# Small contexts of two batches at once, in attention over pooled keys followed by a mixture of experts

## The chip, the cores and the metric

The kernel runs on one core of one Trainium2 chip. The metric is the time of one execution on the device, in microseconds (us). The core's engines are TensorE (PE; its weight loads are shown as PEld), VectorE (DVE), ScalarE (ACT), GpSimd (POOL) and SyncE (SP). Each works through its own instructions in order, and semaphores tie them together. PE writes to PSUM, which has eight banks; a bank holds 512 float32 columns on each of 128 partitions.

## The reference

Attention over pooled keys and values, then a dense mixture of experts over all tokens.

```python
# attention: batch 8, heads 8, sequence 576, head size 64, pooled by 8 to 72 keys
k_p = k.reshape(B, H, Sp, pool, D).mean(axis=3)
v_p = v.reshape(B, H, Sp, pool, D).mean(axis=3)
scores = scale * np.matmul(q, k_p.transpose(0, 1, 3, 2))
attn = np.exp(scores - np.max(scores, axis=-1, keepdims=True))
attn = attn / (np.sum(attn, axis=-1, keepdims=True) + 1e-09)
attn_out = np.matmul(attn, v_p)
...
# mixture: x is attn_out as 4608 tokens x 512, 4 experts, hidden size 1024
p = domain_probs / (domain_probs.sum(-1, keepdims=True) + 1e-09)
for e in range(E):
    h = np.maximum(x @ w1[e], 0.0)
    out += p[:, e:e + 1] * (h @ w2[e])
```

## The kernel before

**Chunks.** A batch has 576 = 512 + 64 queries. The first 512 of each batch make a chunk of 512 tokens, chunks 0 to 7. The last 64 of all eight batches make a ninth, chunk 8, kept in `x_rem`. Every chunk goes through the four experts. For each pair of chunk and expert the up product (512 x 512 by 512 x 1024, then relu) and the down product (512 x 1024 by 1024 x 512, times a probability, added to `acc`) are each done by seven products of half-size matrices, with sums of quarters formed by VectorE (`hidden_sums`, `x_sums`, `combine` at L246).

**Slots.** From chunk 1 on an order written out by hand runs: a loop over slots g (L1072), seven to a pair of chunk and expert, 28 to a chunk. A slot issues, in this order: hidden sums on VectorE; step g % 7 of the up product of unit 0 and step (g - 1) % 7 of that of unit 1 (eight 256-column matmuls at L695 together); step (g - 1) % 7 of the down product of the pair before (eight 256-column matmuls at L763); then the pieces of attention work planned for that slot. With `manual_schedule` each engine keeps this order.

**Banks.** PSUM holds `att` (two banks, for attention), `units` (two units of two banks, for the up product) and `chains` (two banks named o_ps, for the down product). A unit's step 0 is copied by ScalarE from its bank 0 to its bank 1 (L708). Step 1 grows bank 1 and is read by ScalarE's relu (L712), steps 4 and 6 use bank 1 and are read by VectorE (`relu_sum`, L675), steps 2, 3 and 5 use bank 0 and are read by ScalarE (L710, L716). So a unit's bank 1 is not in use between the relu of step 1 and step 4. In the down product step 0's bank is copied by ScalarE to the other (L771), once the adds of the pair before have left that one, and step 1 grows the copy. Most results are added to `acc` by VectorE, two instructions to a step (`add`, L842).

**Attention work.** `pieces_later` (L966) plans it per batch b, counted from slot 28 x (b - 2): for b = 2 its own numbers, for b = 3 to 7 mostly those of `usual`, for b = 8, where only the small part of batches 6 and 7 is left, a variant. `context` (L460) multiplies the exponentials of 128 queries (72 keys x 128 queries as weights) with a head's pooled values and a column of ones (65 columns), for 8 heads, into `att`. `divide` (L424) takes the reciprocal of the ones' column and multiplies.

**The small part.** At every even b from 2 on, for visit i = b // 2 - 1, the 64 last queries of batches 2i and 2i + 1 are handled together. `rem_queries` transposes them by a transfer. `rem_scores` (L496) makes 16 products of 64 columns into `att`, and ScalarE takes the exponential of all at once into `expTr` (L510), a batch at a time: first the four head pairs of one batch, then those of the other. `rem_context` (L513) makes 16 products at L520, one per head and batch, with 64 columns of weights each: the first batch's results go to partitions 0 to 63 of `att`, the second's to 64 to 127. `divide` follows, and `rem_turn` transposes into `x_rem` by a transfer on SP's queue. `usual` puts these four at slots -3, 17, 24 and 25, b = 2 at 0, 7, 8 and 14, b = 8 at -3, 17, 21 and 22. The pooled values of three batches are kept in three tiles `vps`, batch b in number b % 3, written by `values_folds`.

Of the kernel before, what the change touches and what calls it, by code (L numbers as in the profile page):

```python
# [10 lines left out]
ALU = mybir.AluOpType  # L11
AX = mybir.AxisListType
BF16 = mybir.dt.bfloat16
F32 = mybir.dt.float32
# [3 lines left out]
def kernel(  # L18
# [10 lines left out]
    nc = tc.nc  # L29

    B, H, S, D = q.shape
    E, DM, F = moe_w1.shape
    P = nc.NUM_PARTITIONS
    NPAIR = H // 2
    POOL = 8
    SP = S // POOL
    NT = 512
    NR = NT // P
    REM = S - NT
# [8 lines left out]
    const = ctx.enter_context(tc.tile_pool(name="const", bufs=1))  # L48
# [3 lines left out]
    apool = ctx.enter_context(tc.tile_pool(name="apool", bufs=1))  # L52
    xpool = ctx.enter_context(tc.tile_pool(name="xpool", bufs=2))
    npool = ctx.enter_context(tc.tile_pool(name="npool", bufs=2))
# [10 lines left out]
    att = psum.tile([P, 2, NT], F32, name="att")  # L65
    units = [None, None]
# [27 lines left out]
    SPT = -(-SP // 16) * 16  # L94
    kp_all = const.tile([SPT, H, 2, D], BF16, name="kp")
    kpTs = [const.tile([P, H + 1, SPT], BF16, name=f"kpT{i}") for i in range(3)]
    vps = [const.tile([SP, H, D + 1], BF16, name=f"vp{i}") for i in range(3)]
    raw_k = rawpool.tile([SP, H, 2, D], BF16, name="kraw")
    raw_v = rawpool.tile([SP, H, 2, D], BF16, name="vraw")

# [89 lines left out]
    def load_q_rem(b):  # L190
        if b % 2 == 0:
            q_rems[b // 2] = qpool.tile([P, H, D], BF16, name="q_rem", bufs=2)
        lo = (b % 2) * REM
        nc.gpsimd.dma_start(
            out=q_rems[b // 2][lo:lo + REM],
            in_=q[b, :, NT:S, :].rearrange("h p d -> p h d"),
        )
# [50 lines left out]
    state = {}  # L248
# [22 lines left out]
    def fold_wide(what, part):  # L271
        raw, wide = ((raw_k, wide_k), (raw_v, wide_v))[what]
        a, *others = (wide[:, :, 2 * i:2 * i + 2, :] for i in range(wide.shape[2] // 2))
        if part == 0:
            for other in others:
                nc.vector.tensor_add(out=a, in0=a, in1=other)
        else:
            nc.vector.tensor_add(out=raw[:], in0=raw[:], in1=a)
# [68 lines left out]
    def queries(b):  # L347
        state[("qT", b)] = apool.tile([P, H, 2, P], BF16, name="qT")
        nc.sync.dma_start_transpose(
            out=state[("qT", b)][:].rearrange("p h a t -> p (h a) t"),  # L350
            in_=raws[("q", b)][:].rearrange("p h r d -> p (h r d)"),
        )
# [27 lines left out]
    def key_columns(b, h, lo):  # L380

        h = h if b else h // 2
        return state[("kpT", b)][:].rearrange("p h j -> p (h j)")[lo:lo + D, h * SPT:h * SPT + P]
# [40 lines left out]
    def divide(c_ps, x_tok):  # L424

        n = c_ps.shape[1]
        c = c_ps[:, :, 0:NPAIR * (D + 1)].rearrange("p a (h d) -> p a h d", d=D + 1)
        inv = npool.tile([P, 2, NPAIR], F32, name="inv")[:, 0:n]
        nc.vector.reciprocal(out=inv, in_=c[:, :, :, D])
        nc.vector.tensor_tensor(  # L430
            out=x_tok[:], in0=c[:, :, :, 0:D],
            in1=inv.unsqueeze(3).to_broadcast([P, n, NPAIR, D]), op=ALU.mult,
        )
# [61 lines left out]

    def rem_scores(i):  # L496
        qTr = state.pop(("qTr", i))
        scr_ps = att[:].rearrange("p h (b a t) -> p h b a t", b=2, a=NPAIR)
        for bb in range(2):
            for pair in range(NPAIR):  # L500
                for hh in range(2):
                    lo = hh * D
                    nc.tensor.matmul(
                        scr_ps[:, hh, bb, pair, :],
                        lhsT=key_columns(2 * i + bb, 2 * pair + hh, lo),
                        rhs=qTr[lo:lo + D, pair, bb, :],
                        skip_group_check=True,
                    )
        expTr = apool.tile([SP, 2, 2, NPAIR, REM], BF16, name="expTr")
        nc.scalar.activation(out=expTr[:], in_=scr_ps[0:SP], func=ACT.Exp, scale=EXP_SCALE)  # L510
        state[("expTr", i)] = expTr

    def rem_context(i):  # L513
        expTr = state.pop(("expTr", i))
        x_tok = npool.tile([P, 2, NPAIR, D], BF16, name="x_tok", bufs=4)
        c_ps = att
        for h in range(H):
            at = h % NPAIR * (D + 1)
            for bb in range(2):
                nc.tensor.matmul(  # L520
                    c_ps[bb * REM:(bb + 1) * REM, h // NPAIR, at:at + D + 1],
                    lhsT=expTr[:, h % 2, bb, h // 2, :], rhs=vps[(2 * i + bb) % 3][:, h, :],
                    skip_group_check=True,
                )
        divide(c_ps, x_tok)
        state[("xr", i)] = x_tok

    def rem_turn(i):
# [140 lines left out]
    def x_sum(c, n):  # L669
        if n == 0:  # L670
            state[("x_sums", c)] = x_sums(c)
        state[("x_sums", c)][n]()
# [293 lines left out]
    def pieces_later():  # L966


        at, amid = {0: [lambda: x_sum(1, 3)]}, {}

        def put_amid(slot, piece):
            amid[slot] = piece

        def put(slot, *pieces):
            at.setdefault(slot, []).extend(pieces)

        usual = dict(
            queries=-8, keys=-9, values=-2, scores=((2, 2), (9, 2)), contexts=(11, 14, 18, 21),
            q=1, k=(-2, 0, 5, 9), v=(-2, 0, 5, 9), x=(22, 25, 25, 25), rem=(-3, 17, 24, 25),
        )  # L980
        plans = {b: usual for b in range(BUSY, B + 1)}
        plans[BUSY] = dict(
            queries=0, keys=4, values=12, scores=((9, 2), (12, 1), (15, 1)), contexts=(16, 17, 19, 21),
            q=6, k=(5, 8, 11, 14), v=(13, 16, 19, 26), x=(24, 25, 25, 25), rem=(0, 7, 8, 14),
        )
        plans[B] = dict(usual, x=(24, 24, 25, 25), rem=(-3, 17, 21, 22))
        plans[BUSY + 1] = dict(usual, keys=-8, turned=-6, values=4, v=(5, 8, 12, 16))

        for b, plan in plans.items():
            start = 7 * E * (b - BUSY)  # L990

            def put_each(what, pieces):
                for slot, piece in zip(plan[what], pieces, strict=True):
                    put(start + slot, piece)

            if b == BUSY:
                put(start + 1, lambda: fold_wide(0, 0))
                put(start + 4, lambda: fold_wide(0, 1))
                put(start + 5, lambda: load_q_rem(BUSY))
                put(start + 8, lambda: fold_wide(1, 0))  # L1000
                put(start + 12, lambda: fold_wide(1, 1))
            if b < B:
                put(start + plan["queries"], lambda b=b: queries(b))
                put(start + plan["keys"], lambda b=b: fold_keys(b))
                put(start + plan.get("turned", plan["keys"] + (b > BUSY)), lambda b=b: keys(b, every))
                put(start + plan["values"], *values_folds(b))
                pair = 0
                for slot, n in plan["scores"]:
                    if n == 2:
                        put(start + slot, lambda b=b, pair=pair: scores_of_two(b, pair))  # L1010
                        put_amid(start + slot + 1, lambda b=b, pair=pair: scores(b, pair, 1))
                    else:
                        put(start + slot, lambda b=b, pair=pair: scores(b, pair))
                    pair += n

                for r, slot in zip((2, 3, 0, 1), plan["contexts"]):
                    put(start + slot, lambda b=b, r=r: context(b, r))
                    put(start + slot + 1, lambda b=b, r=r: turn(b, r))
            if b + 1 < B:
                put(start + plan["q"], lambda b=b: load_q(b + 1), lambda b=b: load_q_rem(b + 1))  # L1020
                for what in range(2):
                    put_each("kv"[what], [lambda b=b, what=what, part=part: load_part(b + 1, what, part)
                                          for part in range(NR)])
            if b % 2 == 0:
                i = b // 2 - 1
                put_each("rem", [lambda i=i, do=do: do(i)
                                 for do in (rem_queries, rem_scores, rem_context, rem_turn)])
            put_each("x", [lambda b=b, n=n: x_sum(b, n) for n in range(4)])
        return at, amid

    ENG = mybir.EngineType
    with tc.manual_schedule(
# [30 lines left out]

        N = len(order)
        later, amid = pieces_later()
        below_of = [(0, 3)] + order
        sums = {}
# [4 lines left out]
        for g in range(7 * N + 1):  # L1072
            t, i = divmod(g, 7)
# [53 lines left out]
```

## Time and profile before

| what | us |
|---|---|
| median of 3 runs | 489.60 (489.58 to 489.82) |
| the profiled execution | 489.93 |
| its span, from the first to the last instruction | 488.2 |
| PE busy in the span | 480.5 (98%) |
| PEld, DVE, ACT, POOL busy | 409.4, 376.9, 303.8, 119.4 |
| the four small contexts L520 start at | 82.4, 216.4, 319.8, 415.7 |
| the divisions L430 out of `att`, 33 of them, each | 0.69 |

The granted TensorE clock is 0.999 of the full one. A share of busy time is a mean over the whole execution. In the timelines a row is: start and duration in us, engine, line, operation, the tile written and those read, the shape, the number of instructions merged, and in brackets the idle time in front with what ended it. In the chain of work in order of time a row is start, duration, engine, tile, line and number of instructions; a piece there begins where the one before it ends, so its start lies a little behind that of the timeline. The shape of a matmul is weights, rows x columns, then the moving operand, rows x columns.

### The profile page before, as it was taken

The numbers are of one execution on the slowest core, as the hardware profiler recorded it, in microseconds if no ns is written. First come the engines' busy times: TensorE is split into PE (matmuls) and PEld (weight loads), VectorE is DVE, ScalarE is ACT, GpSimd is POOL, SyncE is SP. The second block draws the span as 40 slices with busy tenths as digits, with TensorE's granted clock in tenths as the row PEclk, the third lists the DMA queues.
The fourth block names the chain that finished last, engine by engine and source line by source line (L and its number), as shares of the span: only waits on it lengthen the run. The fifth ranks groups of instructions, "written<-read, shape, count | busy, mean of one in ns | idle before, by whom it ended". The sixth has DMA issues, their size and how long they took to land.

```text
span 488.2 us, 11522 instructions
## 1 busy us (share of the span) xinstructions
PE 480.5 (98%) x4673; PEld 409.4 (84%) x4678; DVE 376.9 (77%) x758; ACT 303.8 (62%) x576; POOL 119.4 (24%) x120
## 2 busy tenths in 40 slices
PE   8999999999999999999999999999999999999996
PEld 4669568898888888888888888888898888888885
DVE  4779799989768976798679866997678766876674
ACT  5677446855676567656765567556755567556650
POOL 8520504242523154016321442111011101010000
PEclk9999999999999999999999999999999999999999
DMA  9999999994986489345954298311111010004003
GB/s 195 203 209 203 204 170 155 103 90 54 110 110 63 77 86 137 35 83 56 159 50 91 27 165 66 68 23 66 35 23 23 23 64 3 12 23 87 1 1 87
DMA packets 104996, 41.96 MB, mean 86 GB/s; under 512 B 75504, under 2 KB 104432, under 8 KB 104944
## 3 DMA queue, kind: packets, MB, share of 16 engines
q0 software_dynamic: 58496, 22.35, 41.8%
q1 hardware_dynamic: 45328, 17.84, 16.7%
q10 hardware_dynamic: 1120, 1.05, 0.6%
q8 instruction: 36, 0.59, 0.5%
q14 instruction: 16, 0.13, 0.1%
HBM read 45.69 MB, written 9.44 MB: 113 GB/s over the span
## 4 chain that ended last, share of the span: by engine, by line
PE 91%; DMA 3%; ACT 2%; DVE 2%; POOL 1%; issue 1%; POOLq 0%; ACTq 0%
PE unit L695 42%; PE o_ps L763 41%; DMA w_bf<-in_moe_w_dram 3%; PE att L467 1%; PE unit L822 1%; PE o_ps L617 1%; PE att L393 1%; ACT expT L549 1%; PE unit L617 1%; PE unit L393 0%; DVE wt_bf L246 0%; POOL wt_bf L142 0%; ACT qT L378 0%; DVE acc L842 0%; PE work_first L631 0%
## 5 line engine op out<-in xcount | busy, mean ns | idle before, releaser
L842 DVE SCALAR_TENSOR_TENSOR acc<-o_ps,p_all,acc 128x256 f32<-128x256 f32 (+1 forms) x285 | 126.9, 485 | 52.9 <-PE o_ps L763 36.5
L763 PEld LDWEIGHTS <-H 128*128 128x128 bf16 x1320 | 129.1, 98 | 15.5 <-issue 0.6
L695 PEld LDWEIGHTS <-w_bf 128*128 128x128 bf16 x1088 | 105.2, 98 | 13.0 <-issue 0.2
L675 DVE CUSTOM_DVE_ANT_0 H<-unit,partial 128x512 bf16<-128x512 f32 x128 | 87.2, 684 | 23.8 <-ACT partial L710 11.5
L763 PE MATMUL o_ps<-w_bf,H 128*128 128x256 bf16 x792 | 102.6, 273 | 0.4 <-ACT o_ps L771 0.4
L695 PE MATMUL unit<-xT,w_bf 128*128 128x256 bf16 x704 | 100.5, 273 | 0.0
L777 POOL TENSOR_TENSOR acc<-acc,addend 128x512 f32<-128x512 f32 x24 | 30.7, 1279 | 253.2 <-ACT addend L775 202.2
L710 ACT COPY partial<-unit 128x512 f32<-128x512 f32 x128 | 72.3, 592 | 30.2 <-PE unit L695 30.2
L695 PEld LDWEIGHTS <-wu_bf 128*128 128x128 bf16 x816 | 77.6, 98 | 11.7 <-issue 2.5
L695 PE MATMUL unit<-xs,wu_bf 128*128 128x256 bf16 x512 | 77.0, 273 | 0.0
L763 PE MATMUL o_ps<-wt_bf,H 128*128 128x256 bf16 x528 | 68.4, 273 | 0.0
L712 ACT ACTIVATE H<-unit 128x512 bf16<-128x512 f32 x66 | 39.8, 605 | 30.9 <-PE unit L695 30.9
L763 PEld LDWEIGHTS <-S 128*128 128x128 bf16 x528 | 51.7, 98 | 6.0
L716 ACT ACTIVATE H<-unit 128x512 bf16<-128x512 f32 x66 | 39.6, 602 | 25.6 <-PE unit L695 25.3
L708 ACT COPY unit<-unit 128x512 f32<-128x512 f32 x68 | 39.4, 582 | 23.6 <-PE unit L695 18.0
L695 PE MATMUL unit<-xs,w_bf 128*128 128x256 bf16 x256 | 38.4, 273 | 0.0
L840 ACT ACTIVATE acc<-o_ps,p_all 128x256 f32<-128x256 f32 x72 | 30.7, 485 | 9.4 <-PE o_ps L763 7.7
L152 POOL DMA_DIRECT2D kraw<-in_k_dram x20 | 26.3, 1317 | 39.0 <-DMA kraw<-in_k_dram 39.0
L695 PE MATMUL unit<-xT,wu_bf 128*128 128x256 bf16 x240 | 35.7, 272 | 0.0
L763 PE MATMUL o_ps<-w_bf,S 128*128 128x256 bf16 x264 | 34.2, 273 | 0.0
L763 PE MATMUL o_ps<-wt_bf,S 128*128 128x256 bf16 x264 | 34.2, 273 | 0.0
L152 POOL DMA_DIRECT2D vraw<-in_v_dram x20 | 28.4, 1420 | 18.8 <-DMA vraw<-in_v_dram 18.5
(162 smaller groups left out, 500.2 us busy)
## 6 DMA issues: line engine op xcount, KB each, us to landing
out_dram<-acc SPq DMA_DIRECT2D x32, 256.0 KB, 4.2
w_bf<-in_moe_w_dram POOLq DMA_DIRECT2D x10, 512.0 KB, 17.4
q_sb<-in_q_dram POOLq DMA_DIRECT2D x7, 512.0 KB, 9.6
vraw<-in_v_dram POOLq DMA_DIRECT2D x22, 144.0 KB, 6.5
kraw<-in_k_dram POOLq DMA_DIRECT2D x21, 144.0 KB, 5.7
w_bf<-in_moe_w_dram POOLq DMA_DIRECT2D x2, 1024.0 KB, 17.8
w_bf<-in_moe_w_dram POOLq DMA_DIRECT2D x4, 256.0 KB, 7.3
wt_bf<-in_k_dram POOLq DMA_DIRECT2D x4, 144.0 KB, 5.4
```

The lines of the kernel that those rows point to most:

```text
L152: nc.gpsimd.dma_start(out=raw[:], in_=rows_of(src, b, 2 * part, 2 * part + 2), accum_op=ALU.add if part else ALU.bypass)
L617: nc.tensor.matmul(out_ps, lhsT=w1_bf[:, e, kc, fc * P:(fc + 1) * P], rhs=xT[:, kc, at], start=(kc == 0), stop=(kc == KC - 1), skip_group_ ...
L675: nc.vector._custom_dve(TENSOR_ADD_SAT, out=dst, in0=ps, in1=part, s0=LARGEST, s1=0.0)
L695: nc.tensor.matmul(ps[:, n * HN:(n + 1) * HN], lhsT=lhs[:, kc, f:f + P], rhs=rhs[:, kc, :], start=(not grows and n == 0 and kc == 0), stop ...
L708: nc.scalar.copy(out=banks[1][:], in_=ps)
L710: nc.scalar.copy(out=part[:, step - 2], in_=ps)
L712: nc.scalar.activation(out=quarter(0, 0), in_=ps, func=ACT.Relu)
L716: nc.scalar.activation(out=quarter(0, 1), in_=ps, func=ACT.Relu)
L763: nc.tensor.matmul(ps[:, j], lhsT=lhs[:, i, j * P:(j + 1) * P], rhs=rhs[:, i, :], start=(not grows and i == 0 and j == 0), stop=(i == HF - 1),
L777: nc.gpsimd.tensor_add(out=dst, in0=dst, in1=addend[:])
L840: nc.scalar.activation(out=dst, in_=o_ps, func=ACT.Copy, scale=prob)
L842: nc.vector.scalar_tensor_tensor(out=dst, in0=o_ps, scalar=prob, in1=dst, op0=ALU.mult, op1=ALU.add,)
```

## The change

In visits 1 to 3, not in visit 0, `rem_context_whole` takes the place of `rem_context`. For each head it makes one product: the weights are the 128 exponentials of both batches' queries side by side, and the moving operand is the two batches' values for that head, 2 x 65 columns out of the one tile that now holds all three. So each of the 128 rows of the result holds both batches' values, one of which belongs to it. Heads 0 to 5 go to `att`, heads 6 and 7 to bank 1 of unit 1. The division is done for each bank group, heads 6 and 7 first, and for each half of the partitions by itself: two reciprocals and four products, where `divide` has one and one. `rem_scores` writes the exponentials with the two batches of a head next to each other. In the plans the small context and its transposition go from slots 24 and 25 to 23 and 24 for b = 4 and 6; for b = 8 scores, context and transposition go from 17, 21 and 22 to 10, 17 and 18.

```diff
-    vps = [const.tile([SP, H, D + 1], BF16, name=f"vp{i}") for i in range(3)]
+    vp_all = const.tile([SP, 3, H, D + 1], BF16, name="vp")
+    vps = [vp_all[:, i] for i in range(3)]
...
-        scr_ps = att[:].rearrange("p h (b a t) -> p h b a t", b=2, a=NPAIR)
+        scr_ps = att[:].rearrange("p h (a b t) -> p h a b t", b=2, a=NPAIR)
...
-                        scr_ps[:, hh, bb, pair, :],
+                        scr_ps[:, hh, pair, bb, :],
...
-        expTr = apool.tile([SP, 2, 2, NPAIR, REM], BF16, name="expTr")
+        expTr = apool.tile([SP, 2, NPAIR, 2, REM], BF16, name="expTr")
...
-                    lhsT=expTr[:, h % 2, bb, h // 2, :], rhs=vps[(2 * i + bb) % 3][:, h, :],
+                    lhsT=expTr[:, h % 2, h // 2, bb, :], rhs=vps[(2 * i + bb) % 3][:, h, :],
...
+    def rem_context_whole(i):
+
+        expTr = state.pop(("expTr", i))
+        x_tok = npool.tile([P, 2, NPAIR, D], BF16, name="x_tok", bufs=4)
+        of = [(2 * i + bb) % 3 for bb in range(2)]
+        low, high = sorted(of)
+        parts = [(att[:], 0, H // 2 - 1), (units[1][1][:].unsqueeze(1), H - 2, 2)]
+        parts = [(h0, n, bank[:, :, 0:n * 2 * (D + 1)].rearrange("p a (h b d) -> p a h b d", h=n, d=D + 1))
+                 for bank, h0, n in parts]
+        for h0, n, c in parts:
+            for a in range(c.shape[1]):
+                for hh in range(n):
+                    h = h0 + a * n + hh
+                    nc.tensor.matmul(
+                        c[:, a, hh], lhsT=expTr[:, h % 2, h // 2].rearrange("j b t -> j (b t)"),
+                        rhs=vp_all[:, low:high + 1:high - low, h, :], skip_group_check=True,
+                    )
+        inv = npool.tile([P, 2, NPAIR], F32, name="inv")[:].rearrange("p a h -> p (a h)")
+        x = x_tok[:].rearrange("p a h d -> p (a h) d")
+        for h0, n, c in reversed(parts):
+            hs = slice(h0, h0 + c.shape[1] * n)
+            over = inv[:, hs].rearrange("p (a h) -> p a h", h=n)
+            nc.vector.reciprocal(out=over, in_=c[:, :, :, 0, D])
+            for bb in range(2):
+                ps = slice(bb * REM, (bb + 1) * REM)
+                nc.vector.tensor_tensor(
+                    out=x[ps, hs].rearrange("p (a h) d -> p a h d", h=n),
+                    in0=c[ps, :, :, of.index(low) ^ bb, 0:D],
+                    in1=over[ps].unsqueeze(3).to_broadcast([REM, c.shape[1], n, D]), op=ALU.mult,
+                )
+        state[("xr", i)] = x_tok
...
-            q=1, k=(-2, 0, 5, 9), v=(-2, 0, 5, 9), x=(22, 25, 25, 25), rem=(-3, 17, 24, 25),
+            q=1, k=(-2, 0, 5, 9), v=(-2, 0, 5, 9), x=(22, 25, 25, 25), rem=(-3, 17, 23, 24),
...
-        plans[B] = dict(usual, x=(24, 24, 25, 25), rem=(-3, 17, 21, 22))
+        plans[B] = dict(usual, x=(24, 24, 25, 25), rem=(-3, 10, 17, 18))
...
-                                 for do in (rem_queries, rem_scores, rem_context, rem_turn)])
+                                 for do in (rem_queries, rem_scores,
+                                            rem_context_whole if i else rem_context, rem_turn)])
```

## The prediction

> **What bounds the kernel.** I read the page's chain that ended last, then that chain in order of time around the visit at 216 us (batch 4), then the timelines of VectorE and ScalarE there, and last the groups with their shapes apart.
>
> ```profile
> PE 91%; DMA 3%; ACT 2%; DVE 2%; POOL 1%; issue 1%; POOLq 0%; ACTq 0%
> ```
>
> The chain in order of time (start, us, what), an ordinary context and then the small one:
>
> ```profile
> 205.45 0.26 PE att L467 x8
> 205.71 0.88 PE unit L695 x8
> ...
> 215.58 0.87 PE o_ps L763 x8
> 216.46 0.38 PE att L520 x16
> 216.84 0.98 PE unit L695 x8
> 217.81 0.22 PE o_ps L763 x2
> ```
>
> Every block of eight 256-column products takes 0.87, and the next begins at once: PE waits for nobody here. So only PE's own work, or a new wait of PE, moves the end. The small context costs more than its 0.38: the block behind it takes 0.98 for 0.87. A visit is worth 0.38 + 0.11 = 0.49. The ordinary context (72x128 weights) costs 0.26 and leaves the next block at 0.88: no switch.
>
> VectorE around that visit (slots 24 to 28), then ScalarE's copy of one o_ps bank into the other:
>
> ```profile
> 215.61 0.68 DVE L246 TENSOR_TENSOR H<-H,S 128x1024 bf16<-128x1024 bf16 x1
> 216.49 0.87 DVE L842 SCALAR_TENSOR_TENSOR acc<-o_ps,p_all,acc 128x256 f32<-128x256 f32 x2 [0.20 <-PE o_ps L763]
> 217.29 0.19 DVE L429 RECIPROCAL inv<-att 128x8 f32<-128x8 f32 x1
> 217.51 0.69 DVE L430 TENSOR_TENSOR x_tok<-att,inv 128x512 bf16<-128x512 f32 x1
> 218.12 0.68 DVE L675 CUSTOM_DVE_ANT_0 H<-unit,partial 128x512 bf16<-128x512 f32 x1
> ...
> 223.26 0.68 DVE L246 TENSOR_TENSOR S<-H 128x1024 bf16<-128x1024 bf16 x1
> 223.86 0.68 DVE L675 CUSTOM_DVE_ANT_0 H<-unit,partial 128x512 bf16<-128x512 f32 x1
> 224.46 0.86 DVE L842 SCALAR_TENSOR_TENSOR acc<-o_ps,p_all,acc 128x256 f32<-128x256 f32 x2
> ```
>
> ```profile
> 225.71 0.57 ACT L771 COPY o_ps<-o_ps 128x512 f32<-128x512 f32 x1 [0.16 <-PE o_ps L763]
> ```
>
> VectorE has almost no gap from 215.6 to 226.5. Its adds of slot 28 end at 225.32; the copy L771 starts at 225.71, held by PE and not by VectorE, and PE's next step needs that copy at 226.38. So VectorE is hidden with some 0.3 us to spare. The trace shows once, near 70 us, what happens when it is not:
>
> ```profile
> 69.08 0.74 DVE L842 SCALAR_TENSOR_TENSOR acc<-o_ps,p_all,acc 128x512 f32<-128x512 f32 x1
> ...
> 69.91 0.57 ACT L771 COPY o_ps<-o_ps 128x512 f32<-128x512 f32 x1 [0.77 <-DVE acc L842]
> ...
> 70.53 0.71 PE L763 MATMUL o_ps<-w_bf,H 128*128 128x256 bf16 x5 [0.39 <-ACT o_ps L771]
> ```
>
> An add that ends late (69.82) lets the copy begin 0.09 later, it takes 0.57, and PE starts 0.05 after it.
>
> **The change, part by part.**
>
> *PE, three visits.* Removed: 3 x 0.49. Added: 3 x 8 products of 130 columns with 72x128 weights, which no row has. Eight of 65 columns take 0.26 (0.033 each), eight of 256 take 0.87 (0.109). A 130-column product lies between 0.033 and 2 x 0.033 = 0.066; the line through the 256-column row (0.43 ns a column) gives 0.056, and I take that: 0.45 a visit, bounds 0.26 and 0.53. As in L467 I expect no switch on either side. Gain 0.04 a visit, 0.11 in all (0.68 gained to 0.12 lost).
>
> *PE elsewhere.* The scores write the same 64 columns to other places, the first visit reads the same 64 weights columns elsewhere: nothing. The one tile for three value tiles adds no wait that binds: a batch's values are written at slot 4, 12 or -2, long before or after a reader.
>
> *VectorE, three visits.* Removed: a reciprocal (0.19) and a division of 512 columns (0.69), from 217.29 to the next start at 218.12: 0.83. Added: two reciprocals and four products on 64 partitions (2 x 128 and 2 x 384 columns). Reciprocals: 8 columns take 0.20 and 36 columns 0.378 (the group L239), 6.4 ns a column: 0.16 and 0.19. Products: a PSUM read of 128 columns takes 0.286 (the cast L333), of 512 columns 0.691; between them 384 columns take 0.556, and 128 take 0.29. A product starts 0.03 after its reciprocal's end (217.29 + 0.19, then 217.51).
>
> Between instructions that wait for nothing VectorE overlaps: the pair of adds at 216.49 takes 0.87 where its two last 0.478 each, so 0.08 are shared. But the only pair in the trace where the second writes from partition 64 on does not:
>
> ```profile
> 4.85 1.01 DVE L246 TENSOR_TENSOR S<-S 64x648 bf16<-64x648 bf16 x2 [1.11 <-POOL S L110]
> ```
>
> Two of 0.498 take 1.01: the second starts 0.01 after the first ends. The next one, back at partition 0, starts 0.03 after (5.86 to 5.89), though that could be a wait of its own. The new visit changes half four times: down to up twice, back twice. I take 0.01 after the end at all four. A visit is then 0.16 + 0.03 + 0.29 + 0.01 + 0.29 + 0.01 + 0.19 + 0.03 + 0.56 + 0.01 + 0.56 + 0.01 = 2.15. Bounds: 1.78 if all four overlap (0.09 less each); 3.21 if every product took 0.69 as the whole one does.
>
> [...]
>
> *Where it lands, batches 4 and 6.* The visit now follows the adds of slot 23, so it starts at 215.61. Behind it VectorE has, start to start: hidden sum 0.60, adds 0.79, relu sum 0.60, adds 0.79, three x sums 1.00, relu sum 0.60, values 0.34, relu sum 0.60, adds 0.79, hidden sum 0.60, relu sum 0.60, which is 7.31 without a gap; all their inputs are ready by then. The adds of slot 28 start at 215.61 + 2.15 + 7.31 = 225.07 and end at 225.93 instead of 225.32. Then 0.09, the copy's 0.57 and 0.05: PE may go on at 226.64. It would want to at 226.38 - 0.04 = 226.34. Stall 0.30. What is queued behind: on ScalarE the next partial copies, on PE everything. Earlier deadlines in that stretch (the o_ps bank of step 2 free by 219.37, the unit banks by 220.2 and 222.4) are met or cost part of the same 0.30. It decides from a visit of 1.85 on. Batch 6 repeats batch 4 with every number 103.44 later: 2 x 0.30.
>
> *Batch 8, slot 17.* No contexts, values or x sums follow. The visit starts at 409.15 behind the adds of 408.36; the relu sum L675 behind it ends at 409.15 + 2.15 + 0.68 = 411.98, and its bank is wanted by PE at 412.09: met by 0.06 after the 0.05 of handing over. Nothing. The scores moved to slot 10 cost the same 0.34 there, and their exponential (1.02 on ScalarE) has room where the other batches have 2.2 of it. The transposing transfers move with their visits; on SP's queue nothing stands behind them before the stores, ten us later, and x_rem is read only by the last chunk.
>
> Sum: 0.60 - 0.11 = +0.49. The profiled execution took 489.93 (span 488.2 and 1.7 around it), so 490.42; the median of the runs lies 0.33 below it, so **490.1**.
>
> **The rivals.**
>
> - *VectorE overlaps anyway.* A visit of 1.78 keeps under 1.85; what is left is PE's 0.11: 489.5. For: every pair of full-height instructions overlaps. Against: the pair at 4.85.
> - *Slower by more: changing half is dearer.* The memset of kp (partitions 64 to 79) starts at 3.26 though the one before ended at 3.12: 0.14 instead of 0.01. With 0.14 at all four a visit is 2.67; stalls of 0.82 twice, and in batch 8 the relu sum ends 0.46 too late: +1.99, so 491.6. It decides from 2.33 on, where the sum passes 1 us. The dearest bound, 3.21, gives 2 x 1.36 + 1.0 - 0.11: 493.2. Against: the instructions in front of that memset are too short (0.07) to say what held it.
> - *PE gains more.* If 130 columns streamed as fast as 65 the gain is 0.68: 489.5 with my stall, 488.9 without. Against: 256 columns cost 3.3 times 65.
> - *It doesn't do what it says: the second bank isn't free.* Heads 6 and 7 write unit bank 1 of unit 1, read by ScalarE's relu L712 of slot 23, which ends at 214.57; the seventh product is due at 214.55 + 6 x 0.056 = 214.89. Only a ScalarE that ran 0.3 late would stall PE; one further instruction of 0.6 would cost 0.3 a visit: 491.0.
>
> **How the numbers follow.** The forecast 0.50 (its own range 489.8 to 490.4), overlap kept 0.18, dearer halves 0.22, a larger gain on PE 0.04, the bank 0.06. A measurement of this kernel can't tell less than about 0.2%, 1 us, from no change. The forecast and the kept overlap stay within that, and so do two thirds of the bank's case: same 0.72. Dearer halves and the rest of the bank: slower 0.24. Faster 0.04. The range goes from 489.3, under the kept overlap, to 491.3, into the slower cases.
>
> **What would show it.** Right: at the three later visits L467-like products of 130 columns with no idle before them and 0.87 behind them; half-height products that start after their predecessor's end; a VectorE visit of about 2.15; once after each of the visits of batches 4 and 6 an idle PE before L763, released by ScalarE's L771, of about 0.3; none near 412. Wrong: starts before the end (no stall at all), products of over 0.6, idle time of PE before the small context, or a stall put down to anything but L771 or the L708 copy just before it.

## The result, and the profile after

The changed kernel takes 491.77 us (491.03 to 493.47, 6 runs), the one before beside it 489.80 (489.58 to 490.14, 6 runs): a ratio of 1.0040 with a 95% interval of 1.0027 to 1.0052, about 2 us slower. The profiled execution took 491.83 with a span of 489.8; the one before 489.93 with 488.2. So 1.6 of the difference lie within the span.

The chain in order of time at the visit of batch 4, as it was shown for the kernel before (L728 is the up product, L796 the down product, L542 the new one):

```profile
213.67 0.87 PE o_ps L796 x8
214.54 0.35 PE att L542 x6
214.89 0.11 PE unit L542 x2
215.00 0.88 PE unit L728 x8
```

The eight products of 130 columns take 0.46 (0.35 + 0.11) and the block behind them 0.88, so PE loses nothing at the change to these products and back. PE's own part of the change came as it was meant to. The time was lost 10 us later. This is PE's timeline there, then ScalarE's:

```profile
222.77 1.04 PE L796 MATMUL o_ps<-wt_bf,H 128*128 128x256 bf16 x8
224.33 1.03 PE L728 MATMUL unit<-xT,w_bf 128*128 128x256 bf16 x8 [0.53 <-ACT unit L741]
```

```profile
223.71 0.57 ACT L741 COPY unit<-unit 128x512 f32<-128x512 f32 x1 [1.89 <-DVE H L708]
...
226.48 0.57 ACT L804 COPY o_ps<-o_ps 128x512 f32<-128x512 f32 x1 [0.21 <-DVE acc L875]
```

A block of eight starts every 0.87 us when nothing waits. From 222.77 to 224.33 are 1.56, so 0.69 are lost, and PE was released by ScalarE's copy of a unit's bank 0 to bank 1, which itself waited for VectorE's relu sum. A second copy, of an o_ps bank, waited for VectorE's adds and cost PE 0.15 more; 0.07 had been lost at 219.28. That is 0.91 behind the visit of batch 4, and the same again behind that of batch 6. Before, there was none. VectorE's timeline between the visit and the second copy:

```profile
215.44 0.16 DVE L551 RECIPROCAL inv<-unit 128x2 f32<-128x2 f32 x1
215.63 0.59 DVE L554 TENSOR_TENSOR x_tok<-unit,inv 64x128 bf16<-64x128 f32 x2
216.26 0.20 DVE L551 RECIPROCAL inv<-att 128x6 f32<-128x6 f32 x1
216.49 1.12 DVE L554 TENSOR_TENSOR x_tok<-att,inv 64x384 bf16<-64x384 f32 x2
217.64 0.69 DVE L247 TENSOR_TENSOR H<-H,S 128x1024 bf16<-128x1024 bf16 x1
218.35 0.88 DVE L875 SCALAR_TENSOR_TENSOR acc<-o_ps,p_all,acc 128x256 f32<-128x256 f32 x2
...
221.52 0.68 DVE L708 CUSTOM_DVE_ANT_0 H<-unit,partial 128x512 bf16<-128x512 f32 x1
222.12 0.90 DVE L343 TENSOR_TENSOR vp<-vraw 72x512 bf16<-72x512 bf16 x1
222.94 0.68 DVE L708 CUSTOM_DVE_ANT_0 H<-unit,partial 128x512 bf16<-128x512 f32 x1
...
225.53 0.86 DVE L875 SCALAR_TENSOR_TENSOR acc<-o_ps,p_all,acc 128x256 f32<-128x256 f32 x2
```

The visit lasts from 215.44 to 217.64, 2.20 against a forecast of 2.15. But the values' sum L343 (`values_folds`) takes 0.90, where the kernel before needed 0.415 at this place:

```profile
221.54 0.41 DVE L342 TENSOR_TENSOR vp<-vraw 72x512 bf16<-72x512 bf16 x1
```

Of the six such sums only those of batches 5 and 7, right behind the two visits, are long; the other four take 0.41 to 0.43. GpSimd's timeline, after and then before, points to a cause, which the experiments then test:

```profile
221.38 1.36 POOL L810 TENSOR_TENSOR acc<-acc,addend 128x512 f32<-128x512 f32 x1 [11.81 <-DVE xT L247]
```

```profile
221.50 1.58 POOL L777 TENSOR_TENSOR acc<-acc,addend 128x512 f32<-128x512 f32 x1 [11.77 <-ACT addend L775]
```

After, the sum starts 0.75 behind the start of GpSimd's add and ends at 223.02, 0.28 after the add's end at 222.74. Before, it started at 221.54, only 0.04 behind the add's start; then the sum kept its 0.415, and the add was the longer one, 1.58 for its usual 1.26. In both traces the add starts 0.13 after ScalarE has ended its `addend`; the bracket of after names an x sum of VectorE that ended 0.02 later than that.

### The profile page after: what moved, and what is told of

It reads as the page before. It is cut to its first block, busy times and chain, and to the rows that moved or that the text cites. A ratio compares the mean times of both kernels' runs of the same rounds, so it can differ in the third digit from the quotient of the medians.

```text
span 489.8 us, 11493 instructions
## 1 busy us (share of the span) xinstructions
PE 481.2 (98%) x4654; PEld 408.8 (83%) x4654; DVE 380.8 (78%) x770; ACT 303.6 (62%) x576; POOL 119.2 (24%) x120
## 4 chain that ended last, share of the span: by engine, by line
PE 86%; DMA 8%; POOL 2%; DVE 2%; issue 0%; ACT 0%; POOLq 0%; ACTq 0%
PE unit L728 40%; PE o_ps L796 39%; DMA wt_bf<-in_v_dram 5%; DMA w_bf<-in_moe_w_dram 3%; PE o_ps L822 2%; PE att L468 2%; PE unit L855 1%; POOL w_bf L208 1%; POOL wt_bf L143 1%; PE att L394 1%; DVE H L708 0%; PE unit L394 0%; DVE vp L343 0%; DVE wt_bf L269 0%; PE att L504 0%
## 5 line engine op out<-in xcount | busy, mean ns | idle before, releaser
L796 PEld LDWEIGHTS <-H 128*128 128x128 bf16 x1320 | 128.6, 98 | 16.0 <-issue 0.3
L728 PEld LDWEIGHTS <-w_bf 128*128 128x128 bf16 x1088 | 104.9, 98 | 14.6 <-issue 1.6
L708 DVE CUSTOM_DVE_ANT_0 H<-unit,partial 128x512 bf16<-128x512 f32 x128 | 87.2, 684 | 23.6 <-ACT partial L743 11.5
L796 PE MATMUL o_ps<-w_bf,H 128*128 128x256 bf16 x792 | 102.6, 273 | 0.0
L728 PE MATMUL unit<-xT,w_bf 128*128 128x256 bf16 x704 | 100.5, 273 | 1.0 <-ACT unit L741 1.0
L728 PEld LDWEIGHTS <-wu_bf 128*128 128x128 bf16 x816 | 77.5, 98 | 11.8 <-issue 2.5
L728 PE MATMUL unit<-xs,wu_bf 128*128 128x256 bf16 x512 | 77.0, 273 | 0.0
L796 PE MATMUL o_ps<-wt_bf,H 128*128 128x256 bf16 x528 | 68.4, 273 | 0.0
L796 PEld LDWEIGHTS <-S 128*128 128x128 bf16 x528 | 51.5, 98 | 6.2
L741 ACT COPY unit<-unit 128x512 f32<-128x512 f32 x68 | 39.3, 581 | 26.1 <-PE unit L728 16.6
L728 PE MATMUL unit<-xs,w_bf 128*128 128x256 bf16 x256 | 38.4, 273 | 0.0
L728 PE MATMUL unit<-xT,wu_bf 128*128 128x256 bf16 x240 | 35.7, 273 | 0.0
L796 PE MATMUL o_ps<-wt_bf,S 128*128 128x256 bf16 x264 | 34.2, 273 | 0.0
L796 PE MATMUL o_ps<-w_bf,S 128*128 128x256 bf16 x264 | 34.2, 273 | 0.0
```

The costliest lines, as they stand in the source:

```text
L708: nc.vector._custom_dve(TENSOR_ADD_SAT, out=dst, in0=ps, in1=part, s0=LARGEST, s1=0.0)
L728: nc.tensor.matmul(ps[:, n * HN:(n + 1) * HN], lhsT=lhs[:, kc, f:f + P], rhs=rhs[:, kc, :], start=(not grows and n == 0 and kc == 0), stop ...
L741: nc.scalar.copy(out=banks[1][:], in_=ps)
L796: nc.tensor.matmul(ps[:, j], lhsT=lhs[:, i, j * P:(j + 1) * P], rhs=rhs[:, i, :], start=(not grows and i == 0 and j == 0), stop=(i == HF - 1),
```

## The experiments

Two questions: is the loss VectorE's lateness or PE's new form and borrowed bank, and is the long sum due to GpSimd's add or to the tile that now holds all three batches' values. Stalls are PE's lost time behind a visit, from start to start. The runs fall into two sets, each on one chip with the kernel before beside it: one_product to half_by_half (its median 489.94), and the rest (489.85).

| kernel | median, us | ratio to before (95% interval) | stall, batch 4 / batch 6 |
|---|---|---|---|
| one_product | 489.70 | 0.9998 (0.9990 to 1.0007) | 0 / 0 |
| old_products | 492.08 | 1.0042 (1.0030 to 1.0054) | 0.87 / 0.87 |
| values_later | 490.69 | 1.0014 (1.0004 to 1.0024) | 0.42 / 0.42 |
| half_by_half | 491.20 | 1.0025 (1.0016 to 1.0034) | 0.75 / 0.75 |
| both | 489.64 | 0.9994 (0.9985 to 1.0003) | 0 / 0 |
| after_again | 491.86 | 1.0037 (1.0023 to 1.0051) | 0.91 / 0.91 |
| one_sum_more | 491.24 | 1.0027 (1.0018 to 1.0037) | 1.06 / 0 |

**one_product.** The new products with a division in one piece per bank.

```diff
-            for bb in range(2):
-                ps = slice(bb * REM, (bb + 1) * REM)
-                nc.vector.tensor_tensor(out=x[ps, hs]..., in0=c[ps, :, :, of.index(low) ^ bb, 0:D], in1=over[ps]...)
+            nc.vector.tensor_tensor(out=x[:, hs]..., in0=c[:, :, :, of.index(low), 0:D], in1=over...)
```

> The changed kernel with each bank's division as one product over all 128 partitions instead of one for each half. It leaves out the choice of the batch: the upper half gets the lower batch's values. VectorE theory (the loss comes from VectorE's longer visit and what it pushes back): the visit falls from 2.20 us to some 1.1, under the 1.85 from which a stall begins; no idle PE at the copies, PE keeps its 0.04 a visit: 0.1 us under the kernel before. Rival, PE or the banks (the whole products, the borrowed unit bank or the strided operand cost it): the 0.91 of idle PE behind each of the visits of batches 4 and 6 stays, 1.6 to 2 us over the kernel before.

The visit took 1.10 (215.80 to 216.90), no copy behind the visits made PE wait, and the time is that of the kernel before within the interval. (In the profiled execution PE lost 0.35 once, at 110.9, ahead of all three changed visits; no other trace shows it, and its cause is not known.) PE's new form, the borrowed bank and the strided operand cost nothing that can be told.

**old_products.** The other part alone: the old 16 products, but a division in halves.

```diff
-                                            rem_context_whole if i else rem_context, rem_turn)])
+                                            rem_context, rem_turn)])
...
-        divide(c_ps, x_tok)
+        if i == 0:
+            divide(c_ps, x_tok)
+        else:
+            ...
+            for a in range(2):
+                nc.vector.reciprocal(out=inv[:, a], in_=c[:, a, :, D])
+                for bb in range(2):
+                    ps = slice(bb * REM, (bb + 1) * REM)
+                    nc.vector.tensor_tensor(out=x_tok[ps, a], in0=c[ps, a, :, 0:D], in1=inv[ps, a]..., op=ALU.mult)
```

> The changed kernel with the 16 old half-width products in all visits, in the new slots, but the division in two reciprocals and four half-height products of 256 columns (about 2.2 us of VectorE, as in the changed kernel). VectorE theory: about 0.9 of stall at each of the visits of batches 4 and 6, and PE's 0.49 a visit back: 1.7 to 1.9 us over the kernel before. Rival, PE or the banks: no loss beyond noise, within 0.3 us of the kernel before.

The whole loss is there without the new products: 2.1 us over the kernel before (1.5 to 2.6 by the interval), 0.87 a visit, the values' sums of batches 5 and 7 at 0.89 each. So the longer division, not PE's part, makes the kernel slower.

**values_later.** The values leave the slot of GpSimd's add.

```diff
-            queries=-8, keys=-9, values=-2, ...
-            q=1, k=(-2, 0, 5, 9), v=(-2, 0, 5, 9), ...
+            queries=-8, keys=-9, values=-1, ...
+            q=1, k=(-2, 0, 5, 9), v=(-1, 0, 5, 9), ...
```

> The changed kernel with the values of batches 4 to 7 formed one slot later (27 for 26), behind the down product's adds; the first load of the next values behind it. Theory of the two engines (the values' sum reads two operands from SBUF while GpSimd's add runs, and waits for its end: 0.9 us instead of 0.42): the sum takes 0.42 again in batches 5 and 7, the stall per visit falls from 0.91 to about 0.43, all of it at the copy from one o_ps bank to the other: 1.0 us under the changed kernel, 0.6 to 0.8 over the one before. Rival, the common tile (its layout slows the write): the sum stays at 0.9, and with it the stall at 0.9.

VectorE's timeline:

```profile
221.24 1.28 DVE L708 CUSTOM_DVE_ANT_0 H<-unit,partial 128x512 bf16<-128x512 f32 x2
222.44 0.86 DVE L875 SCALAR_TENSOR_TENSOR acc<-o_ps,p_all,acc 128x256 f32<-128x256 f32 x2
223.22 0.42 DVE L343 TENSOR_TENSOR vp<-vraw 72x512 bf16<-72x512 bf16 x1
```

With the same tile and the same layout the sum takes 0.42 again, behind an add of GpSimd's that ended at 222.44. The stall is 0.42 for an expected 0.43, though not all of it at the copy between the o_ps banks: 0.07 falls early, 0.35 there. The layout is out.

**half_by_half.** Fewer changes of half, everything else as in the changed kernel.

```diff
+        groups = []
         for h0, n, c in reversed(parts):
             ...
             nc.vector.reciprocal(out=over, in_=c[:, :, :, 0, D])
-            for bb in range(2):
+            groups.append((hs, n, c, over))
+        for bb in range(2):
+            for hs, n, c, over in groups:
                 ps = slice(bb * REM, (bb + 1) * REM)
                 nc.vector.tensor_tensor(
```

> The changed kernel with the same instructions of the division in another order: both reciprocals, both products of the lower half, both of the upper, so that the half changes twice and not four times. The visit falls from 2.20 us to about 1.77. Theory of the two engines: the values' sum of batches 5 and 7 starts 0.43 earlier, but still within GpSimd's add, and ends when it ended before; the stall stays at 0.85 to 0.91 a visit and the time within 0.2 us of the changed kernel. Rival, the common tile or any cost that just adds up on VectorE: every visit gains 0.43, 0.8 us under the changed kernel.

The visit, from VectorE's timeline, and the values' sum, then GpSimd's add:

```profile
215.66 0.16 DVE L552 RECIPROCAL inv<-unit 128x2 f32<-128x2 f32 x1
215.74 0.17 DVE L552 RECIPROCAL inv<-att 128x6 f32<-128x6 f32 x1
215.85 0.28 DVE L557 TENSOR_TENSOR x_tok<-unit,inv 64x128 bf16<-64x128 f32 x1
216.06 0.54 DVE L557 TENSOR_TENSOR x_tok<-att,inv 64x384 bf16<-64x384 f32 x1
216.61 0.30 DVE L557 TENSOR_TENSOR x_tok<-unit,inv 64x128 bf16<-64x128 f32 x1
216.83 0.55 DVE L557 TENSOR_TENSOR x_tok<-att,inv 64x384 bf16<-64x384 f32 x1
217.41 0.69 DVE L247 TENSOR_TENSOR H<-H,S 128x1024 bf16<-128x1024 bf16 x1
...
221.90 1.19 DVE L343 TENSOR_TENSOR vp<-vraw 72x512 bf16<-72x512 bf16 x1
```

```profile
221.53 1.27 POOL L813 TENSOR_TENSOR acc<-acc,addend 128x512 f32<-128x512 f32 x1 [11.74 <-ACT addend L811]
```

Read the starts: the two lower products overlap (216.06 begins before 215.85 + 0.28), the first upper one begins 0.01 after the end at 216.60, the two upper ones overlap again. The visit is 1.75, 0.45 shorter, but the sum just grows to 1.19 and ends at 223.09, again 0.28 after GpSimd's add (221.53 + 1.27 = 222.80). Of the 0.45 gained, 0.16 reach PE: the 0.07 at 219.28 is gone, and the add is 0.09 shorter (1.27 for 1.36). In the changed kernel, and in values_later with its add of 1.35, an x sum of VectorE ran 0.23 into the add; here none does. So the stall is 0.75 where 0.85 to 0.91 was expected. In the medians this kernel and the changed one, which ran in the other set, lie 0.7 apart with overlapping intervals, so there the expectation, 0.2, is neither met nor refuted. The 1.19 is as the theory has it: the sum started 0.37 instead of 0.75 behind the add's start and still ended 0.28 after its end.

**both.** The edits of half_by_half and values_later together.

> The changed kernel with both edits: the products half by half, and the values of batches 4 to 7 one slot later. Theory of the two engines: the visit of 1.77 us keeps under the 1.85 from which a stall begins and the values' sum is out of GpSimd's add: no idle PE at the copies, 0.0 to 0.2 us under the kernel before (PE keeps 0.02 a visit), 1.6 to 2 us under the changed one. Rival (the lost time lies around the span or in something else that the change brought): a loss over 0.5 us against the kernel before stays.

No stall; 0.06% under the kernel before with an interval that holds 1. It takes the loss away, all of it, but it doesn't beat the kernel before by anything that can be told.

**after_again** is the changed kernel unchanged, in the second set.

> The changed kernel as it is, beside the others on the same chip: 1.4 to 2.2 us over the kernel before, with 0.9 us of idle PE behind each of the visits of batches 4 and 6.

It took 2.0 us over the kernel before, with the 0.91 behind each of the two visits.

**one_sum_more.** The wait without the change: the kernel before, with one instruction of 0.33 twice more.

```diff
+                if b in (5, 7):
+                    put(start + plan["values"], lambda b=b: x_sum(b - 1, 3))
                 put(start + plan["values"], *values_folds(b))
```

> The kernel before with one instruction of VectorE more in each of two slots: the last x sum of batches 4 and 6 (0.33 us) is formed a second time in slot 26, just ahead of the values. Theory of the two engines: in batch 4 the second sum takes the place 0.04 behind the start of GpSimd's add, the values start 0.37 behind it and wait for its end, 1.4 us in place of 0.42; VectorE is late by 1.4, and PE stalls by some 1.1. In batch 6 the values start as GpSimd's add does, are not held, and the 0.33 is hidden. 0.9 to 1.2 us over the kernel before. Rival (an instruction costs what it lasts): 0.33 is hidden both times, no difference.

VectorE in batch 4, then in batch 6, then GpSimd in batch 4 and in batch 6:

```profile
221.54 0.41 DVE L246 TENSOR_TENSOR xs<-xT,xs 128x512 bf16<-128x512 bf16 x1
221.87 1.50 DVE L342 TENSOR_TENSOR vp<-vraw 72x512 bf16<-72x512 bf16 x1
...
325.68 0.41 DVE L246 TENSOR_TENSOR xs<-xT,xs 128x512 bf16<-128x512 bf16 x1
326.01 0.42 DVE L342 TENSOR_TENSOR vp<-vraw 72x512 bf16<-72x512 bf16 x1
```

```profile
221.50 1.59 POOL L777 TENSOR_TENSOR acc<-acc,addend 128x512 f32<-128x512 f32 x1 [11.77 <-ACT addend L775]
...
325.99 1.56 POOL L777 TENSOR_TENSOR acc<-acc,addend 128x512 f32<-128x512 f32 x1 [11.76 <-ACT addend L775]
```

One instruction of 0.33 costs PE 1.06 in batch 4 and nothing in batch 6. What differs is where VectorE stands against GpSimd's add: in batch 4 the values' sum starts 0.37 behind the add's start and ends at 223.37, 0.28 after its end; in batch 6 it starts 0.02 behind and takes 0.42, and the add takes 1.56. This kernel has separate value tiles and the old contexts, so neither the common tile nor the new products are needed for the long sum. The median is 1.4 over the kernel before (0.9 to 1.8 by the interval), for 0.9 to 1.2 expected; the profiled span is 1.0 longer.

## Why the prediction was wrong

It forecast 490.1; the measured 491.77 lies above its range. The step that failed is the one that put VectorE's work behind the visit, "start to start", at "7.31 without a gap", and in it one term: the values at 0.34. That length was taken from the trace of before, where the sum stood elsewhere against GpSimd's add; the runs showed 0.82 in its place, because the later sum had to wait for that add.

- *PE's own cost.* Forecast 0.45 a visit for the new products, measured 0.46; no switch on either side, as forecast. The gain is 0.02 a visit, not 0.04.
- *VectorE's visit.* Forecast 2.15, measured 2.20. The next instruction starts 0.01 after the end at each of the two changes to the upper half, and 0.03 after it at each of the two back, as the rows at 4.85 and 5.89 did in the trace of before. For the way back the 0.01 was the author's estimate, since the wait at 5.89 could have been one of its own; in these runs the overlap was lost in both directions. In the visit of one_product, where no half changes, each instruction starts 0.08 or 0.09 before the end of the one in front, but for a product, which starts 0.04 after its reciprocal's end; half_by_half loses the overlap at its two changes of half, 216.61 (0.01 after the end) and 217.41 (0.03), and at the adds behind the second (0.02), where no half changes (see the last section).
- *The stretch behind it.* 7.31 forecast from the visit's end to the adds of slot 28, 7.89 measured (217.64 to 225.53). The values' sum took 0.82 from start to start instead of 0.34, which is 0.48 of the 0.58 missing; the hidden sum right behind the visit took 0.71 instead of 0.60, because the adds behind it lost their overlap too. With the visit's 0.05 that is 0.63 more lateness, and the stall became 0.91 instead of 0.30 (0.61 more). The 0.48 is shown: values_later takes it away, and the stall falls by 0.49.
- *Where it bites.* Forecast: the copy L771 (L804 now), or the L708 copy (L741 now) just before it. Measured: 0.15 at the copy L804 at 226.48, and 0.69 at an L741 copy that is not the one just before it (225.69) but the one before that, at 223.71. The prediction's own list of signs counts such a stall as wrong. The mechanism is the one that was priced from the row at 69.9: VectorE late, ScalarE's copy late, PE waits.
- *Batch 6.* The prediction took batch 6 for batch 4 with every number 103.44 later. That is so for PE, but in the kernel before VectorE's values' sum stands 0.35 earlier there (324.63 for 221.54 + 103.44 = 324.98), 0.31 ahead of GpSimd's add. The difference is a gap of 0.35 that VectorE has at 219.15 in batch 4 and not in batch 6. In the changed kernel, whose longer visit leaves no such gap, PE lost 0.90 behind the visit of batch 6 all the same.
- *Batch 8.* No stall, as forecast; no values are formed there. The moved scores and transfers cost nothing.
- *The sum.* 0.91 + 0.90 less PE's 0.06 is 1.75. The span grew by 1.6; up to the scores of batch 4 (203.02 for 203.19), ahead of all three changed visits, this execution was already 0.17 ahead.
- *The rivals.* "Changing half is dearer" gave 491.6 and came close to the time, for a reason that is refuted: it needed a visit of 2.67. "VectorE overlaps anyway" is refuted by the starts, "PE gains more" by the 0.46, which would have had to be 0.26. The borrowed bank is cleared by one_product.

A sign of the missing term stood in the trace of before. GpSimd's add at 221.50 took 1.58 where the other 23 take 1.26 or 1.27, and the values' sum began 0.04 behind its start. By the prediction's own times the sum would move to 222.14 (215.61 + 2.15, and 4.38 of its list ahead of the values), inside an add that lasts from 221.50 to some 222.76. The prediction did not look at GpSimd, though its add is timed by PE and ScalarE, and the change moves VectorE against it. That the sum would be the one to wait was not shown there: at 221.50 the add was recorded first, and yet the sum, 0.04 behind, kept its 0.415 and the add was the longer one. Priced as a wait for the rest of the add, 0.62 by these times and no more than an estimate, the delay makes a stall of 0.92, and the sum would have come to 489.6 + 2 x 0.92 - 0.11 = 491.3. The runs agree in kind: with rests of 0.61, 0.91 and 1.21 the sums took 0.90, 1.19 and 1.50, which is 0.48, 0.77 and 1.08 more than 0.42, each ending 0.28 after the add.

## What to carry to other kernels

When a change makes an engine late, slide its whole later timeline against the other engines' and look for pairs that used to miss each other: here a late VectorE ran into an add of GpSimd that PE and ScalarE time, and a forecast lateness of 0.6 us (225.93 for 225.32) became 1.2 (226.39, in an execution 0.17 ahead). A saving on the bound engine (0.06 us in all here) has to be set against the slack of the engines it hands work to; the trace shows that slack where the hidden chain last meets the bound one. Two edits are worth trying elsewhere: products on one half of the partitions grouped by half (here a visit of 1.75 for 2.20), and a VectorE sum kept out of GpSimd's adds (here the values' sum 0.42 for 0.90). Together they took the whole loss away here, 489.64 beside 489.85 for the kernel before.

## What was not expected of the hardware

- Which of the two engines waits wasn't settled by the recorded starts alone, and either lost. A VectorE sum that started 0.02 or 0.04 behind GpSimd's add ran at its own 0.42 and stretched the add to 1.56 and 1.58; one at 0.37 behind was itself stretched, by 0.77 and 1.08. No run lies between 0.04 and 0.37. An estimate: sums that ran 0.46, 0.44, 0.23 and 0.10 into an add (at 221.50 before, 325.99 in one_sum_more, 221.38 after, 324.94 before) made it 0.32, 0.30, 0.09 and 0 longer, which is as if GpSimd's add were in the way only from 0.14 behind its recorded start.
- The relu sum at 221.52, which has one operand in PSUM and one in SBUF, was not held: it started 0.15 after the add's start and took its usual 0.68.
- The instruction two behind a change of half started late as well: the adds at 218.35 start 0.01 after the hidden sum's end (217.64 + 0.69 rounded), without the usual overlap of 0.08, in half_by_half too (218.12 after 217.41 + 0.69), though neither stands on the upper half. Behind the visit of batch 8 this does not happen: there a relu sum follows the visit (413.39, 0.69 long) and the adds behind it start at 414.00, 0.08 before its end. The hidden sum reads SBUF alone, so the adds are the first instruction behind the upper products to read PSUM; the relu sum reads PSUM itself. What held the adds is not shown: no run tried it by itself.
